# Batch 3's local q and k turned by DMA instead of the matrix engine, strided rows loaded in two pieces each, and a rearranged order of loads in a fused attention and MLP kernel

## The chip, the cores and the metric

The kernel runs on one core of a Trainium2 chip. The core has a matrix engine (PE, with its weight loads shown as PEld), two engines for elementwise work (DVE and ACT), a general engine that here mostly issues loads (POOL), an engine that here issues stores and DMA transposes (SP), and 16 DMA engines that move all of the data. The metric is the device time of one execution in microseconds (us); lower is better. Before the change it is 300.25 us, the median of three runs (299.5 to 300.93).

## The reference: strided sparse attention, then an MLP

The inputs q, k and v have the shape (8 batches, 8 heads, 576 positions, 64). Heads 0 to 3 are local: a position sees itself and the 31 before it. Heads 4 to 7 are strided: a position sees those at or before it that have the same remainder by 32, at most 18 of them. The attention's output is regrouped into 4608 tokens of 512 numbers, and goes through relu squared between two matrices.

```python
mask_local = (rel >= 0) & (rel < stride)
mask_strided = (rel >= 0) & (pos[None, :] % stride == pos[:, None] % stride)
...
attn = exp(where(mask, q @ k^T / 8, -1e9) - max);  out = (attn / sum) @ v
x = out.transpose(0, 2, 1, 3).reshape(4608, 512)
h = x @ w_in            # 512 x 2048
y = (relu(h) ** 2) @ w_out   # 2048 x 512
```

## The kernel before

**The MLP is the backbone.** The 4608 tokens are cut into 9 chunks of 512. For each chunk there are 16 groups of `mm1` (line 707: four matmuls of 128x128 on 512 columns, then relu on ACT and the square on DVE into `g_sb`) and 16 groups of `mm2` (line 729: four matmuls of 128x128 on 512 columns; every fourth ends an output tile that ACT copies to `y` and SP stores). That makes 288 groups, numbered through. The attention of a batch must be done, and its output stand in the `xt` tiles, before the `mm1` groups of the chunks that hold its tokens.

**The attention is woven in by hand.** The string `PLAN` says which attention steps are emitted ahead of which group, as `group: words`; a batch's two local head pairs are units 4b and 4b+1. The words that matter here:

- `l3k12+13`, `l3q12+13` (line 281): load the local k or q of batch 3, both units in one DMA, in rows of 1536 bytes, into room in `xt` that is not needed yet. `c12kv` and the like (line 294) copy one unit's rows into a `k_l` or `q_l` tile on DVE (`v`) or ACT (`a`). `T12ka` and the like (line 448) transpose them with six matmuls against an identity (line 453) and copy the result out of PSUM (line 460).
- `Q16k`, `Q16q` (line 273): load one unit's k or q straight into `k_l` or `q_l`, in two DMAs, in rows of 256 bytes. `Y16` (line 370) then transposes q and k with two DMA transposes that SP issues (line 378). Batches 4 to 7 go this way; batches 0 to 3 go the way of `l`, `c` and `T`.
- `C4q`, `C4k` (line 346): load the strided heads of a batch, 72 rows of 8 KB. `X4q`, `X4k` (line 352) transpose them by DMA from SP (line 354). `k40v`, `k41v` (line 361) copy the transposed k into the block-diagonal tile `kb` on DVE.
- `V4` (line 412) loads the local v of a batch into 128 partitions, 96 rows of each block and once more the 32 rows ahead of it, so that each block has its neighbours at hand. `U4` (line 388) loads the strided v in two DMAs: 54 rows of 8 KB for three heads (line 390), and 54 rows of 3 KB for the fourth (line 393), whose source is a three-level pattern. `B40v`, `B41v` (line 396) spread that into the tile `vb`.
- `S12!`, `D12.0`, `E12`: scores, the product with v, and the DMA transpose of the result into `xt` for a local unit. `G4` is the scores of both local units of a batch at once. `s3.0` and `x3.0` are scores and product with v for the strided heads.

**What sets the order.** Every engine runs its instructions in the order in which they are emitted, and waits where an operand isn't there. POOL issues all loads, in one line; SP issues all stores and DMA transposes, in one line. The tile framework gives the loads eight semaphores in turn, and the DMAs of SP eight others, so that a load isn't issued before the one eight places ahead of it has landed. Buffers: four `q_l`, four `k_l`, one `q_t` and one `k_t` for the strided rows (the next batch's `C` waits until the DMA transpose has read the last), one `v_st`, four `y`.

Of the kernel before, what the change touches and what calls it, by code (L numbers as in the profile page):

```python
# [82 lines left out]
77: s3.2  # L83
80: x3.0 B40v
81: B41v
82: x3.1
# [10 lines left out]
104: Y21 s4.1  # L97
105: D17.0
106: Q25k
107: B50v  # L100
# [6 lines left out]
116: x4.2  # L107
121: G5
124: V6
128: U6  # L110
133: D20.0
134: Y24 D20.1 X6k
# [8 lines left out]
144: x5.0  # L121
146: x5.1
149: x5.2
150: k60v
152: k61v
154: G6
156: V7
# [13 lines left out]
183: x6.2  # L141
188: G7 k70v
189: k71v
197: s7.0
198: D28.0 s7.1
199: D29.0
# [10 lines left out]
def kernel(  # L157
# [18 lines left out]
    NJ = 8  # L176
# [6 lines left out]
    NG = 5  # L183
# [116 lines left out]
    NP3 = 4 * SP_ // QL  # L300
    str_rows = {}

    def load_str_rows(b, name):
        src = q if name == "q" else k
        if b == 0:
            c = 4 if name == "q" else 8
            t = w_out_b[0:QL, c:c + NP3, :]
            nc.gpsimd.dma_start(out=t, in_=src[b, 4:8].rearrange("h (p j) d -> (h p) (j d)", j=NJ)
                                .rearrange("(s p) c -> p s c", p=QL))
        else:  # L310
            t = str_rows_t[name][0:SP_]
            nc.gpsimd.dma_start(out=t, in_=src[b, 4:8].rearrange("h (m r) d -> (h m) (r d)", r=STRIDE))
        str_rows[b, name] = t

    def step_TS(b, name, g, copy):
# [30 lines left out]
    def load_str_tall(b, name):  # L346
        src = q if name == "q" else k
        t = str_rows_t[name]
        nc.gpsimd.dma_start(out=t[0:SP_], in_=src[b, 4:8].rearrange("h (m r) d -> (h m) (r d)", r=STRIDE))  # L349
        big[b, name] = t  # L350

    def transpose_str(b, name):
# [252 lines left out]

    def load_v0():
        load_v_local_sw(0)
        nc.gpsimd.dma_start(
            out=vs0.rearrange("p u n d -> p (u n d)").rearrange("p (h c) -> p h c", h=4),
            in_=v[0, 4:8].rearrange("h (p j) d -> p h (j d)", j=NJ))  # L610

    def step_N(u):
        e, hw = st[u]["e"], S // 2
# [154 lines left out]
    def first_part(kks, ffs):  # L768
        for ff in ffs:
            mm1(0, ff, kks, FIRST, None if ff < 2 else "py")  # L770

    def run_step(word):
        word, _, at = word.partition("/")
        places[:] = [int(x) for x in at.split(",") if x]
        op, arg = word[0], word[1:]
# [206 lines left out]
```

## Time and profile before

| what | value |
|---|---|
| time, median of three runs (range) | 300.25 us (299.5 to 300.93) |
| time of the profiled execution | 298.88 us |
| its span, first to last instruction | 297.2 us |
| PE busy | 289.2 us, 97% |
| DVE, ACT, POOL busy | 177.9, 172.3, 72.4 us |
| granted PE clock | full over the span but for its last slices (0.96 from 290 us on) |
| DMA moved | 37.28 MB in 93131 packets |
| loads issued by POOL, DMAs issued by SP | 66 and 53 |

The profiled execution took 298.88 us, of which 297.2 us are its span and 1.7 us lie around it. A group of four matmuls takes about 0.865 us at full rate (216 ns from one start to the next). Group 16 starts at 33.3 us of the span, group 48 at 67.8, group 64 at 84.5, group 90 at 110.9.

### The profile page before, as it was taken

Reading aid. Unit: us, or ns where it says so; the run is one execution under the profiler, and the core shown is the slowest. Engines: PE = TensorE matmul, PEld = TensorE weight load, DVE = VectorE, ACT = ScalarE, POOL = GpSimd, SP = SyncE. Lnnn points to the kernel's source line nnn. Section 1 sums busy time; section 2 is a strip of 40 time slices with the busy share of each in tenths; the row PEclk is TensorE's granted clock in tenths of the full one; section 3 lists DMA queues with packets and bytes.
Section 4 is the critical chain, followed back from the end, with each engine's and each line's share of the span. In section 5 each row is a group of like instructions: output and inputs, shape, how many; then the busy total and the mean of one; then the engine's idle time right before and its main releaser. Section 6 shows DMA issues by size and latency. Waiting matters only on the chain.

```text
span 297.2 us, 5652 instructions
## 1 busy us (share of the span) xinstructions
PE 289.2 (97%) x2136; PEld 146.0 (49%) x2172; DVE 177.9 (60%) x460; ACT 172.3 (58%) x325; POOL 72.4 (24%) x105
## 2 busy tenths in 40 slices
PE   7999999999999999999999999999999999999996
PEld 2644555555544444544455445544554444444444
DVE  6866779677779694697267936785475534104400
ACT  3858846686667735783477447745665257217511
POOL 8846643006404027083303710000000000000000
PEclk9999999999999999999999999999999999999999
DMA  8999999999999999999999999521011100010012
GB/s 157 181 209 204 194 198 187 158 225 140 129 166 176 157 211 164 159 136 157 186 145 150 174 186 142 89 57 71 35 23 55 73 35 0 35 74 35 0 71 73
DMA packets 93131, 37.28 MB, mean 125 GB/s; under 512 B 78956, under 2 KB 87238, under 8 KB 93104
## 3 DMA queue, kind: packets, MB, share of 16 engines
q0 software_dynamic: 54448, 18.82, 58.1%
q1 hardware_dynamic: 38512, 18.03, 32.6%
q8 instruction: 17, 0.28, 0.4%
q14 instruction: 10, 0.08, 0.1%
q10 hardware_dynamic: 144, 0.07, 0.1%
HBM read 38.21 MB, written 9.44 MB: 160 GB/s over the span
## 4 chain that ended last, share of the span: by engine, by line
PE 92%; DVE 3%; ACT 2%; issue 2%; DVEq 0%; ACTq 0%
PE psb L729 39%; PE psb L707 39%; PE psb L667 2%; PE psb L453 1%; PE psb L764 1%; PE psb L588 1%; PE psb L505 1%; PE psb L754 1%; PE psb L585 1%; PE psb L574 1%; ACT r L713 1%; PE psb L550 1%; DVE g_sb L714 1%; PE psb L475 1%; PE psb L331 0%
## 5 line engine op out<-in xcount | busy, mean ns | idle before, releaser
L707 PE MATMUL psb<-xt,w_in_b 128*128 128x512 bf16 x558 | 132.1, 379 | 1.4 <-ACT xt L692 0.4
L729 PE MATMUL psb<-w_out_b,g_sb 128*128 128x512 bf16 x542 | 125.3, 379 | 1.3 <-issue 0.6
L713 ACT ACTIVATE r<-psb 128x512 bf16<-128x512 f32 x144 | 85.5, 600 | 37.5 <-PE psb L707 34.0
L714 DVE TENSOR_TENSOR g_sb<-r 128x512 bf16<-128x512 bf16 x144 | 60.7, 423 | 72.8 <-ACT r L713 71.7
L707 PEld LDWEIGHTS <-w_in_b 128*128 128x128 bf16 x576 | 53.4, 98 | 59.0 <-issue 1.6
L729 PEld LDWEIGHTS <-g_sb 128*128 128x128 bf16 x560 | 51.8, 98 | 57.2 <-DVE g_sb L714 0.3
L733 ACT COPY y<-psb 128x512 f32<-128x512 f32 x35 | 20.6, 589 | 53.2 <-PE psb L729 50.2
L598 DVE TENSOR_TENSOR xt<-psb,rv 64x144 bf16<-64x144 f32 x84 | 34.1, 406 | 8.0 <-ACT rv L591 6.8
L590 ACT ACTIVATE rv<-psb 128x432 f32<-128x432 f32 (+1 forms) x21 | 10.5, 501 | 9.8 <-PE psb L585 9.8
L673 DVE TENSOR_TENSOR x_l<-psb,rinv 96x384 bf16<-96x384 f32 x28 | 15.5, 554 | 1.0
L349 POOL DMA_DIRECT2D q_t<-in_q_dram x6 | 3.4, 567 | 43.4 <-DMA qT_s<-q_t 26.0
L604 DVE TENSOR_TENSOR xt<-psb,rv 64x270 bf16<-64x270 f32 (+1 forms) x28 | 10.9, 432 | 3.8 <-ACT rv L591 3.6
L575 ACT ACTIVATE e<-psb 128x432 bf16<-128x432 f32 (+1 forms) x21 | 10.4, 496 | 3.7 <-PE psb L574 3.7
L418 POOL DMA_DIRECT2D vl<-in_v_dram x7 | 10.3, 1475 | 8.6 <-DMA vl<-in_v_dram 6.2
L278 POOL DMA_DIRECT2D k_l<-in_k_dram x16 | 11.7, 736 | 2.8 <-PE psb L453 2.4
L278 POOL DMA_DIRECT2D q_l<-in_q_dram x16 | 11.6, 732 | 1.0 <-DMA k_l<-in_k_dram 1.0
L561 ACT ACTIVATE e<-psb 128x384 bf16<-128x384 f32 x24 | 9.6, 511 | 3.4 <-PE psb L550 3.4
L591 ACT ACTIVATE rv<-rv 128x432 f32<-128x432 f32 (+1 forms) x21 | 11.2, 533 | 0.7
L557 DVE TENSOR_TENSOR e<-e,mask_all 128x576 bf16<-128x576 bf16 x16 | 6.7, 459 | 7.2 <-ACT e L561 7.1
L667 PEld LDWEIGHTS <-e 128*128 128x128 bf16 x168 | 8.6, 101 | 4.6
L349 POOL DMA_DIRECT2D k_t<-in_k_dram x6 | 3.2, 535 | 28.0 <-DMA kT_s<-k_t 25.7
L667 PE MATMUL psb<-vl,e 128*128 128x65 bf16 x168 | 9.5, 195 | 0.1
(117 smaller groups left out, 215.9 us busy)
## 6 DMA issues: line engine op xcount, KB each, us to landing
out_dram<-y SPq DMA_DIRECT2D x35, 256.0 KB, 2.8
vl<-in_v_dram POOLq DMA_DIRECT2D x7, 384.0 KB, 12.4
w_out_b<-in_moe_w_out_dram POOLq DMA_DIRECT2D x4, 512.0 KB, 15.1
q_t<-in_q_dram POOLq DMA_DIRECT2D x7, 288.0 KB, 5.8
k_t<-in_k_dram POOLq DMA_DIRECT2D x7, 288.0 KB, 6.1
v_st<-in_v_dram POOLq DMA_DIRECT2D x7, 216.0 KB, 7.9
w_in_b<-in_moe_w_in_dram POOLq DMA_DIRECT2D x2, 704.0 KB, 13.1
k_l<-in_k_dram POOLq DMA_DIRECT2D x16, 72.0 KB, 8.1
```

What stands on the lines that cost most here:

```text
L278: nc.gpsimd.dma_start(out=t[:, :, hh, :], in_=src[b, 2 * p + hh].rearrange("(t p) d -> p t d", p=QL))
L590: nc.scalar.activation(rv, pn, AF.Ln)
L591: nc.scalar.activation(rv, rv, AF.Exp, scale=-1.0)
L598: nc.vector.tensor_tensor(to[:, :, NJ * part:NJ * (part + 1), par], of, by, op=ALU.mult)
L604: nc.vector.tensor_tensor(t, of[:, g:, :, lo:lo + k], by[:, g:, :, lo:lo + k], op=ALU.mult)
L667: nc.tensor.matmul(po[0:m, n, :], e[:, c:c + m], rhs[:, NL * part + n, 0:D + 1], start=True, stop=True)
L673: nc.vector.tensor_tensor(x, po[0:QL, :, 0:D], rinv[0:QL].to_broadcast([QL, NL, D]), op=ALU.mult)
L707: nc.tensor.matmul(ph, w_in_b[:, kk, 128 * ff:128 * (ff + 1)], xt[kk][:, 512 * c:512 * (c + 1)], start=(kk == order[0]), stop=(kk == order ...
L713: nc.scalar.activation(r, ph, AF.Relu)
L714: later(1, lambda: nc.vector.tensor_tensor(g[:, ff, :], r, r, op=ALU.mult))
L729: nc.tensor.matmul(py, g[:, ff, 128 * j:128 * (j + 1)], w_out_b[:, ff, :], start=(ff == 0), stop=(ff == 15))
L733: nc.scalar.copy(y, py)
```

## The change

Four things are done together.

1. Batch 3's local q and k are loaded with `Q` and transposed with `Y` on SP, as those of batches 4 to 7 are. The steps `l3k`, `l3q`, the four casts `c12*`, `c13*` and the four `T12*`, `T13*` go.
2. A load of 72 or 54 rows becomes two, one of the largest multiple of 16 rows and one of the rest (64 and 8, 48 and 6): `load_even`. The fourth head's v becomes three loads of 18 rows.
3. From batch 3 on the local v is loaded without the shared rows (96 partitions), and DVE copies the 32 rows across (`H3v` to `H7v`).
4. Loads of batch 4 are moved: `Q16*`, `Q17*` from groups 48 to 52 to group 56, behind `C4q`; `U4` from group 63 to 76, where it waits for the DMA transposes of `Y16` (`U4@Y16`); `Y17`, `Y16` from groups 66 and 67 to 76. `X2q` moves from group 31 to 26, ahead of `X2k`. Several steps of batches 3 and 4 shift by a few groups.

```diff
-22: B11v l3k12+13 s1.2 U2
+22: B11v Q12k Q13k s1.2 U2
-26: X2k l3q12+13 x1.1
+26: X2q X2k Q12q Q13q x1.1
-31: c8ka c9qv X2q
+31: c8ka c9qv
+40: Y12
-48: Q16k s2.0
+48: s2.0
-50: Q17q Q16q c12kv s2.1
-51: c12qa E9 s2.2
-52: Q17k c13kv c13qa
+50: s2.1
+51: E9 s2.2
+52: Y13
-56: x2.1 C4k C4q
-57: T12ka
-58: V4 T13qv T12qa
-59: T13ka
-60: x2.2 B30v
-61: B31v
-63: U4 S12!
+56: x2.1 C4q Q16k Q16q C4k Q17k Q17q
+57: H3v
+58: B30v V4
+59: B31v
+60: x2.2
+63: S12!
-66: Y17 k30v
-67: Y16 D12.1 S13! X4k C5q k31v
-68: C5k
-71: s3.0 E12 Q20k Q21q Q20q
-72: Q21k s3.1
-73: D13.0 D13.1
-75: E13
+67: D12.1 S13! C5q
+68: k30v
+69: k31v E12
+70: X4k
+73: D13.0 D13.1 s3.0
+75: s3.1 E13
+76: Y17 Y16 U4@Y16 C5k Q20k Q21q Q20q Q21k
...
+94: H4v
-97: Y20
+97: Y20 B40v Y21
...
+    def load_even(out, src):
+        n = out.shape[0] // 16 * 16
+        for r in (slice(0, n), slice(n, out.shape[0])):
+            nc.gpsimd.dma_start(out=out[r], in_=src[r])
...
-        nc.gpsimd.dma_start(out=t[0:SP_], in_=src[b, 4:8].rearrange("h (m r) d -> (h m) (r d)", r=STRIDE))
+        load_even(t[0:SP_], src[b, 4:8].rearrange("h (m r) d -> (h m) (r d)", r=STRIDE))
...
-        nc.gpsimd.dma_start(out=t[:, 0:RW], in_=v[b, 4:7].rearrange("h (m r) d -> (h m) (r d)", r=STRIDE))
-        src = v[b, 7]
-        src = bass.AP(src.tensor, src.offset, [[2 * NG * D, 3], [RW, NA], [1, 2 * (NG + 1) * D]])
-        nc.gpsimd.dma_start(out=t[:, RW:2 * NB * D], in_=src)
+        load_even(t[:, 0:RW], v[b, 4:7].rearrange("h (m r) d -> (h m) (r d)", r=STRIDE))
+        src = v[b, 7].rearrange("(m r) d -> m (r d)", r=STRIDE)
+        for g in range(3):
+            c = 2 * NG * D * g
+            nc.gpsimd.dma_start(out=t[NA * g:NA * (g + 1), RW:2 * NB * D], in_=src[:, c:c + 2 * (NG + 1) * D])
...
+        word, _, gate = word.partition("@")
...
+                if gate:
+                    tc.add_manual_dep(i, transfers[gate].name,
+                                      mybir.DependencyInfo(mybir.DependencyClass.Sync, mybir.DependencyReason.DATA),
+                                      reason="order of transfers")
...
-            load_v_local_all(int(arg))
+            (load_v_local_sw if int(arg) > 2 else load_v_local_all)(int(arg))
```

More of the change, by code (lines that the diff above doesn't have):

```diff
@@ L59 @@
 47: E8 D9.0 B21v U3
-48: Q16k s2.0
+48: s2.0
 49: D9.1
-50: Q17q Q16q c12kv s2.1
-51: c12qa E9 s2.2
-52: Q17k c13kv c13qa
+50: s2.1
+51: E9 s2.2
+52: Y13
 54: x2.0
 55: X3q X3k
-56: x2.1 C4k C4q
-57: T12ka
-58: V4 T13qv T12qa
-59: T13ka
-60: x2.2 B30v
-61: B31v
-63: U4 S12!
+56: x2.1 C4q Q16k Q16q C4k Q17k Q17q
[4 more added lines that the diff above has]
+63: S12!
 64: X4q
 65: D12.0
-66: Y17 k30v
-67: Y16 D12.1 S13! X4k C5q k31v
-68: C5k
-71: s3.0 E12 Q20k Q21q Q20q
-72: Q21k s3.1
-73: D13.0 D13.1
-75: E13
[L83 to L86, printed above, removed]
+67: D12.1 S13! C5q
[5 more added lines that the diff above has]
+76: Y17 Y16 U4@Y16 C5k Q20k Q21q Q20q Q21k
+78: s3.2
+81: x3.0
+83: x3.1
 85: x3.2
@@ L89 @@
 91: k41v
+94: H4v
 95: U5 D16.0 D16.1
-97: Y20
+97: Y20 B40v Y21
+98: B41v
 99: X5k
@@ L96 @@
 103: C6q s4.0
-104: Y21 s4.1
+104: s4.1
 105: D17.0
@@ L109 @@
 124: V6
+127: H5v
 128: U6
@@ L123 @@
 149: x5.2
-150: k60v
+150: k60v H6v
 152: k61v
@@ L143 @@
 189: k71v
+192: H7v
 197: s7.0
@@ L311, in load_str_rows @@
             t = str_rows_t[name][0:SP_]
-            nc.gpsimd.dma_start(out=t, in_=src[b, 4:8].rearrange("h (m r) d -> (h m) (r d)", r=STRIDE))
+            load_even(t, src[b, 4:8].rearrange("h (m r) d -> (h m) (r d)", r=STRIDE))
         str_rows[b, name] = t
@@ L607, in load_v0 @@
         load_v_local_sw(0)
-        nc.gpsimd.dma_start(
-            out=vs0.rearrange("p u n d -> p (u n d)").rearrange("p (h c) -> p h c", h=4),
-            in_=v[0, 4:8].rearrange("h (p j) d -> p h (j d)", j=NJ))
+        load_even(vs0.rearrange("p u n d -> p (u n d)").rearrange("p (h c) -> p h c", h=4),
+                  v[0, 4:8].rearrange("h (p j) d -> p h (j d)", j=NJ))
     def step_N(u):
@@ L770, in first_part, with run_word @@
             mm1(0, ff, kks, FIRST, None if ff < 2 else "py")
+    transfers = {}
     def run_step(word):
+        word, _, gate = word.partition("@")
+        traced = nc.cur_bb.bb.instructions
+        n = len(traced)
+        run_word(word)
+        for i in traced[n:]:
+            if "DMA" in type(i).__name__.upper() or "Dma" in str(getattr(i, "opcode", "")):
+                transfers[word] = i
+                if gate:
+                    tc.add_manual_dep(i, transfers[gate].name,
+                                      mybir.DependencyInfo(mybir.DependencyClass.Sync, mybir.DependencyReason.DATA),
+                                      reason="order of transfers")
+    def run_word(word):
         word, _, at = word.partition("/")
```

## The prediction

> **What bounds the kernel now.** I read the page's busy shares first, then its slices, then the chain of work that ended last, around the steps that the change removes.
>
> ```profile
> PE 289.2 (97%) x2136; PEld 146.0 (49%) x2172; DVE 177.9 (60%) x460; ACT 172.3 (58%) x325; POOL 72.4 (24%) x105
> PE   7999999999999999999999999999999999999996
> DMA  8999999999999999999999999521011100010012
> PE 92%; DVE 3%; ACT 2%; issue 2%; DVEq 0%; ACTq 0%
> ```
>
> PE is busy in every slice, and 92% of the chain is PE. Busy time alone proves little, so I went through PE's starts in order. A 512-column matmul starts 216 ns after the one before it. From 18 us to the end, nearly every longer step is one extra matmul of 216 ns, of which the trace lacks some records; what is left are some steps of 0.1 to 0.3 us behind score matmuls. So after the head PE waits for nothing, and the kernel gets shorter only by what PE no longer does. Against that, the DMA engines are full until about 190 us: a late load is what can make PE wait. The chain at the removed steps:
>
> ```profile
> 76.19 0.86 PE psb L729 x4
> 77.05 0.26 PE psb L453 x6
> 77.31 0.43 PE psb L729 x2
> ...
> 78.17 0.51 PE psb L453 x12
> 78.68 0.86 PE psb L729 x4
> 79.55 0.26 PE psb L453 x6
> ```
>
> Six transposes take 0.26 us of PE's own line, between matmuls that run back to back. Then the waits, the loads, and SP's line in the crowded stretch:
>
> ```profile
> POOL q_t L349 <- DMA qT_s<-q_t: 26.0, 2, 16.8
> SPq L354 <- DMA k_t<-in_k_dram: 49.9, 1, 49.9
> ...
> v_st<-in_v_dram POOLq DMA_DIRECT2D x7, 216.0 KB, 7.9
> v_st<-in_v_dram POOLq DMA_DIRECT2D x7, 81.0 KB, 8.2
> ...
> 51.73 2.75 SPq L354 DMA_TRANSPOSE kT_s<-k_t  x1
> 54.54 1.58 SPq L737 DMA_DIRECT2D out_dram<-y  x3
> 56.16 4.22 SPq L354 DMA_TRANSPOSE qT_s<-q_t  x1
> ...
> 64.94 0.37 DVE L365 COPY kb<-kT_s 64x864 bf16<-64x864 bf16 x1
> ```
>
> SP waits for batch 2's strided k until 51.7, issues its transpose, three stores, then q's transpose. They land 9.6 and 10.9 us after their starts, at 61.4 and 67.0. DVE wants k at 64.94, PE wants q at 67.6 (`s2.0`). These are the tightest places behind the head. POOL stands 16.8 us for the second transpose, which still reads `q_t`. The small v load takes as long as one 2.7 times its size: its 54 packets of 135 ns run, by their start times, as three rows of 18 one behind the other, so three DMA engines are held 2.4 us while the others are done.
>
> **The change, part by part.**
>
> *Transposes off PE.* `T12*`, `T13*`: 24 matmuls, 0.26 + 0.51 + 0.26 = 1.03 us of the chain. All of it is on the path. Nothing is added on PE. **-1.03 us.**
>
> *Casts and copies.* Four casts (DVE 0.35 each, ACT 0.83 each) and four copies out of PSUM (ACT 0.64 three times, DVE 0.76) go: 4.4 us off engines that are 60% and 58% busy. 0 on the path, since PE wasn't waiting for them.
>
> *Batch 3's loads.* Two of 288 KB become eight of 72 KB. POOL: 8 x 0.73 instead of 0.72 + 0.70, 4.4 us more on an engine 24% busy: 0. In the DMA queue, eight such loads landed between 115.7 and 119.8, 0.58 apart: 4.6 us of queue against about 3.5 for the two (1.7 and 1.8 behind the load before). About 1 us more, around 52 to 60. V3 behind them landed at 68.2 and is first wanted by `H3v` at group 57 (77.1): covered.
>
> *Four DMA transposes on SP.* Each takes 1.2 to 2.0 us to issue by line 378, so 5 to 8 us more in SP's line. `Y12` stands ahead of `E8` (66.9), whose wait for its operand lasts from 61 to 66.9 now: it fits in. `Y13` stands behind the store at 73.0 and ahead of `X3q`, `X3k`, which now start at 73.6 and 77.3 and take 3.6 and 4.6 us because eight `Q16`, `Q17` loads run beside them. Those loads come later in the new order, so I take 1.5 us an issue (lines 354 and 378 take 1.2 to 1.6 where no load runs): Y13, X3q, X3k from 73.5 to about 80, as now. Queued behind are stores; ACT has four `y` buffers and a `y` comes each 3.5 us. `S12!` (group 63, 83.8) and `S13!` (67, 88.1) have over 8 us of cover. 0.
>
> *Loads in pieces.* POOL issues 89 DMAs instead of 66. The nearest rows are 0.51 to 0.65 us an issue: 23 x 0.6 = 14 us, off the path. At the head one piece goes ahead of `w_in`: 0.5 us. The `w_in` loads land 7.9 to 14.7 us after their issue, behind a full queue, and the third lands at 20.6 for group 5 at 21.4: cover of 0.8, so 0. The gain: by the landing counts of each 72-row load one DMA engine is done up to 8 us before the rest and a second up to 4, the others hold five rows of 325 ns. With 64 + 8 that is four each and one more on eight. The 18-row pieces end the chains of 2.4 us. Around 50 us I expect landings 1 to 2 us earlier, bounds 0 and 2.5.
>
> *X2q ahead of X2k.* q landed at 50.0, k at 51.6. With q first the first transpose starts 1.6 us earlier and lands at about 59.8; k's follows without three stores between. Bounds for its landing: 61.4 (as now, when first) and 67.0 (as now, when second). The second one now needs 2.9 us beyond the store before it, so I take 59.8 + 3.5 = 63.3, nearest to the lower. DVE wants it at 64.94; behind that copy stands the mask that ends at 65.85 and that PE needs at 66.52, 0.67 us of cover more. So 0; at the upper end 67.0 - 64.94 - 0.67 = 1.4 us of stall. Below nothing is excluded: PE isn't waiting there now.
>
> *Local v without shared rows.* Five loads shrink by a quarter; each adds one DVE copy of 32x1280, 0.48 us by line 410: 2.4 us on DVE. The nearest deadline is `H3v`, between two long runs of line 598 and ahead of `x2.2`, where DVE has 1.32 us idle at 80.9 and has lost the 0.76 copy: 0.48 and the two `vb` copies moved up (1.04) fit. 0.
>
> *Held back rows.* `Q16`, `Q17` wait behind `C4q`, which waits for `X3q`, some 80 us; they land by about 91. `Y17`, `Y16` then stand behind `E13` (its operand is there at 96): four issues, landed by about 104, for `G4` at 110.9 (109.9 then). `U4` follows at about 104, wanted at group 97 (116.9). Now the last of these transposes lands at 108.2, so the cover grows. 0.
>
> Sum: 298.88 - 1.03 = 297.85 for an execution like the profiled one, span 296.2. The median stands 1.37 above the profiled time (300.25 - 298.88), so **299.2**.
>
> **The rivals.**
>
> *Loads evened out give more.* The median is 1.37 above the profiled execution, and the third and fourth quarter of `w_out` land at 42.9 and 47.0 for groups 24 and 28 at 43.2 and 47.6: an execution with slightly slower DMA would stall there, and the pieces make these landings earlier. If half to all of the 1.37 is such waiting, the time is 297.9 to 298.5; I say 298.2. Against: no trace of such an execution is here.
>
> *X2k late.* Up to 1.4 us of stall at `k20v`: 299.3 to 300.6, as bounded above.
>
> *The eight places run dry: slower.* A load waits for the landing of the one eight ahead, and pieces take places. The third and fourth `w_out` loads were issued at 28.7 and 31.7; now they wait for a piece of k (32.7) and for the second `w_out` load (37.7). If each still took its 14.2 and 15.3 us, the fourth would come at 53.0, 5.4 us after group 28 starts: 300.25 + 5.4 - 1.03 = 304.6. It decides from about 50 us on. Against: landings follow each other by size, not by issue (28.7, 29.5, 31.7 land at 42.9, 44.5, 47.0), and at 37.7 some 1.1 MB still stand in the queue, 6 us of work at 288 KB in 1.7 us.
>
> *Each piece costs a time of its own: slower.* Seven extra pieces stand ahead of or in batch 2's q. At 0.58 us each, as the 72 KB loads, q comes 4.1 us later, X2k at 67.4, and PE stalls 1.8: 301.0. If each held the queue for 3.9 us, the shortest time to landing of any 72 KB load, it is 27 us late and the time some 325. The Trainium skill, DMA: Bandwidth & Descriptors, Rules for kernel authors, speaks for this: small transfers should be merged, and under 64 KB one pays mostly overhead. By the 2.0 us of fixed cost that its section Anatomy of one DMA gives, the seven would be an estimated 14 us. The trace bears it out only where the queue is empty: full, landings come 0.58 us apart.
>
> **How the numbers follow.** Sum as worked out: 0.48 (299.2, and 298.7 to 299.9 by the scatter of the runs). Evened loads give more: 0.26. X2k late: 0.10. The eight places: 0.11. Pieces with a cost of their own: 0.05. A measurement of this kernel can tell about 0.5%, 1.5 us. Faster by over 0.5% is below 298.75: the second case and 0.06 of the first, 0.32. Slower is above 301.75: the eight places and 0.04 of the last, 0.15. Within: 0.53. The range leaves out the slower cases and the lowest edge of the second: 297.9 to 301.4, the upper end being 300.6 for X2k late with 0.7 for the scatter of the median (300.93 - 300.25).
>
> **What would show it.** Line 453's counterpart loses 24 of its 96 matmuls and PE's busy time falls by about 1 us (more by its own durations, which overlap); span near 296.2. Evened loads: strided rows and the fourth head's v land without stragglers, `w_out` no later than 42.9 and 47.0. X2k: k's transpose lands before 65, and DVE shows no wait there for `kT_s`. Wrong would be: a step over 0.3 us between PE's starts behind 18 us, ended by a load or transpose, above all at groups 24 to 28, 44 to 48, 63 and 90.

## The result and the profile after

The changed kernel takes 303.55 us, the median of six executions (301.39 to 305.9), against 299.93 for the kernel before (299.5 to 301.24). The ratio is 1.0116, with a 95% interval of 1.008 to 1.0151: it became slower by 1.2% where I had forecast no change that can be measured. Measured once more with ten executions on another chip it took 302.28 us (299.33 to 304.46) against 300.15. The change also made the time uneven: the executions of one set lie up to 5 us apart, those of the kernel before mostly within 2. The ratios given in this document leave out executions that lie more than 1.5% above the fastest of their kernel; since these late executions are what several of the edits cause, I give the median and the range over all executions, and read from those.

The lines of the page that answer to those shown of before (busy time; PE, granted clock and DMA in 40 slices of the span; shares of the chain that ended last):

```profile
PE 291.1 (97%) x2112; PEld 146.2 (49%) x2148; DVE 180.4 (60%) x462; ACT 169.7 (56%) x320; POOL 92.8 (31%) x147
PE   7799989999999999999999999999999999999995
PEclk9959999999999999999999999999999999999999
DMA  8999999999999999999998996711011110011011
PE 86%; DVE 5%; DMA 3%; ACT 2%; issue 2%; POOL 1%; DVEq 0%; ACTq 0%; POOLq 0%
```

POOL went from 105 instructions to 147: the traces hold 129 loads against 87, so the change adds 42, of which 36 are pieces (the 66 and 53 of the table ahead of the prediction are 87 and 79 in the trace). PE lost its 24 transposes (2136 instructions became 2112), and yet its busy time rose from 289.2 to 291.1: the clock row has a 5 in the third slice, where PE ran at half rate for 6.8 us. PE's share of the chain fell from 92% to 86%; DMA and DVE are on it now. By the starts of the groups, the profiled execution lost 3.5 us up to group 16 (33.35 became 36.87) and 1.0 at group 20, and won 1.0 between groups 56 and 60 (76.0 to 80.8 became 80.5 to 84.3), which are the removed transposes. The other 0.6 us of the span's 4.1 lie behind the landing of the last store.

The loss at the head, from the chain (start, us, what):

```profile
5.54 8.27 DMA vl<-in_v_dram
...
13.84 0.50 DVE vl L420
...
14.37 0.49 PE psb L657 x11
```

Batch 0's local v lands at 13.81 instead of 12.11. The products of line 657 need it: PE stands 0.66 us until it has landed and 0.31 us more for the DVE copy behind it (13.84); another 0.66 us it had stood before, at 8.6, for batch 0's strided k. By 14.7 us PE is 1.6 us behind the kernel before. From 14.8 us on the granted clock is 0.5 for 6.8 us, and at group 5 PE is 3.6 us behind: the halved clock cost 2 us, more than any of the waits.

The loss at group 20, on POOL and then on DVE (start, us, engine, line):

```profile
39.52 0.75 POOL L439 DMA_DIRECT2D w_out_b<-in_moe_w_out_dram  x1 [0.59 <-DMA w_out_b<-in_moe_w_out_dram]
40.26 1.29 POOL L887 MEMSET kb<- 128x1408 f32 x1
```

```profile
39.25 0.38 DVE L374 COPY kb<-kT_s 64x864 bf16<-64x864 bf16 x1
39.55 2.09 DVE L377 COPY kb<-kT_s 64x324 bf16<-64x324 bf16 x1
```

A copy that takes 0.24 us elsewhere takes 2.09 while POOL issues a load and clears `kb`; PE waits 0.83 us for what follows. Before, POOL issued the third and fourth quarter of `w_out` at 28.7 and 31.7 and cleared at 30.2 and 32.4, ahead of these copies; now it does so at 36.1, 39.5, 37.7 and 40.3.

SP's line in the crowded stretch, now with the four new transposes (`qT<-q_l` and `kTl<-k_l` at 67.7 to 79.5):

```profile
67.68 1.22 SPq L387 DMA_TRANSPOSE qT<-q_l  x1
69.01 1.90 SPq L387 DMA_TRANSPOSE kTl<-k_l  x1
71.40 6.00 SPq L691 DMA_TRANSPOSE xt<-x_l  x2
...
78.20 1.23 SPq L387 DMA_TRANSPOSE qT<-q_l  x1
79.47 1.32 SPq L387 DMA_TRANSPOSE kTl<-k_l  x1
80.96 1.32 SPq L363 DMA_TRANSPOSE qT_s<-q_t  x1
82.40 2.09 SPq L363 DMA_TRANSPOSE kT_s<-k_t  x1
...
101.28 3.51 SPq L387 DMA_TRANSPOSE qT<-q_l  x1
104.90 1.22 SPq L387 DMA_TRANSPOSE kTl<-k_l  x1
106.22 1.21 SPq L387 DMA_TRANSPOSE qT<-q_l  x1
107.48 1.27 SPq L387 DMA_TRANSPOSE kTl<-k_l  x1
```

In this execution nothing behind 43 us makes PE wait over 0.35 us. But the last four (batch 4's local rows) land at 109.4 to 110.9, where I had said about 104, and the scores that need them don't wait, starting at 113.8, because PE is 3.5 us late by then. The other executions show what that means.

### The profile page after: what moved, and what is told of

Same layout as the page of the kernel before. It is cut to its first block, busy times and chain, and to the rows that moved or that the text cites. A ratio compares the mean times of both kernels' runs of the same rounds, so it can differ in the third digit from the quotient of the medians.

```text
span 301.3 us, 5671 instructions
## 1 busy us (share of the span) xinstructions
PE 291.1 (97%) x2112; PEld 146.2 (49%) x2148; DVE 180.4 (60%) x462; ACT 169.7 (56%) x320; POOL 92.8 (31%) x147
## 3 DMA queue, kind: packets, MB, share of 16 engines
q1 hardware_dynamic: 40944, 18.62, 32.1%
## 4 chain that ended last, share of the span: by engine, by line
PE 86%; DVE 5%; DMA 3%; ACT 2%; issue 2%; POOL 1%; DVEq 0%; ACTq 0%; POOLq 0%
PE psb L716 38%; PE psb L738 38%; DMA vl<-in_v_dram 3%; PE psb L676 1%; PE psb L598 1%; ACT r L722 1%; PE psb L584 1%; PE psb L763 1%; DVE g_sb L723 1%; PE psb L595 1%; PE psb L560 1%; DVE kb L377 1%; PE psb L698 1%; DVE e L537 1%; DVE kb L374 1%
## 5 line engine op out<-in xcount | busy, mean ns | idle before, releaser
L281 POOL DMA_DIRECT2D k_l<-in_k_dram x20 | 14.8, 746 | 8.1 <-DMA k_t<-in_k_dram 2.2
L281 POOL DMA_DIRECT2D q_l<-in_q_dram x20 | 14.8, 750 | 4.2 <-DMA v_st<-in_v_dram 2.1
L310 POOL DMA_DIRECT2D q_t<-in_q_dram x14 | 7.7, 558 | 26.0 <-DMA qT_s<-q_t 25.5
L310 POOL DMA_DIRECT2D v_st<-in_v_dram x14 | 7.4, 534 | 21.3 <-DVE vb L407 10.7
L614 DVE TENSOR_TENSOR xt<-psb,rv 64x270 bf16<-64x270 f32 (+1 forms) x28 | 10.9, 430 | 2.5 <-ACT rv L601 2.2
L403 POOL DMA_DIRECT2D v_st<-in_v_dram x21 | 10.7, 517 | 4.2 <-DMA w_out_b<-in_moe_w_out_dram 2.3
L310 POOL DMA_DIRECT2D k_t<-in_k_dram x14 | 7.5, 549 | 12.0 <-DMA kT_s<-k_t 7.5
## 6 DMA issues: line engine op xcount, KB each, us to landing
w_in_b<-in_moe_w_in_dram POOLq DMA_DIRECT2D x2, 704.0 KB, 13.3
```

What stands on the lines that cost most here:

```text
L281: nc.gpsimd.dma_start(out=t[:, :, hh, :], in_=src[b, 2 * p + hh].rearrange("(t p) d -> p t d", p=QL))
L310: nc.gpsimd.dma_start(out=out[r], in_=src[r])
L614: nc.vector.tensor_tensor(t, of[:, g:, :, lo:lo + k], by[:, g:, :, lo:lo + k], op=ALU.mult)
```

## The experiments

The times over the kernel before are differences of medians over all executions of the same chip; the last column has the ratio, with its 95% interval, by the rule given above. "Whole" or "pieces" is how the strided rows are loaded; "PE" or "DMA" is how batch 3's local q and k are transposed.

| run | loads | batch 3 | median (range), us | over before, us | ratio (95% interval) |
|---|---|---|---|---|---|
| after_again | pieces | DMA | 302.28 (299.33 to 304.46) | +2.1 | 1.0053 (1.0018 to 1.0088) |
| v0_whole | pieces but for batch 0 | DMA | 303.99 (302.31 to 304.47) | +3.8 | 1.0124 (1.0088 to 1.0159) |
| whole_to_batch1 | pieces from batch 2 | DMA | 302.07 (299.58 to 308.02) | +2.0 | 1.0012 (0.9967 to 1.0056) |
| plan_only | whole | DMA | 304.90 (299.27 to 308.57) | +4.8 | 1.0024 (0.9985 to 1.0063) |
| y_as_before | whole | DMA | 306.85 (300.56 to 313.55) | +6.7 | 1.0070 (1.0020 to 1.0119) |
| y13_behind | whole | DMA | 308.75 (304.14 to 311.63) | +9.1 | 1.0206 (1.0141 to 1.0271) |
| dma_transposes_alone | whole | DMA, old plan | 305.56 (302.56 to 309.62) | +5.4 | 1.0134 (1.0085 to 1.0182) |
| pieces_only | pieces | PE, old plan | 303.58 (301.62 to 304.88) | +3.4 | 1.0115 (1.0061 to 1.0168) |
| pieces_pe | pieces | PE | 301.88 (300.66 to 304.12) | +1.9 | 1.0064 (1.0038 to 1.0091) |
| memsets_first | pieces | PE | 303.42 (302.47 to 303.61) | +3.8 | 1.0110 (1.0087 to 1.0133) |
| tiny_pieces | whole, and tiny extra loads | PE | 301.84 (301.74 to 303.02) | +2.2 | 1.0075 (1.0052 to 1.0098) |
| pe_transposes | whole | PE | 299.48 (299.20 to 300.46) | -0.6 | 0.9987 (0.9971 to 1.0003) |
| rows_only | whole | PE, rows as for DMA | 300.75 (299.31 to 301.30) | +0.8 | 1.0013 (0.9993 to 1.0033) |
| idle_transposes | whole | PE, and four idle DMA | 300.32 (299.43 to 303.81) | +0.4 | 1.0028 (0.9995 to 1.0062) |
| rows_and_idle | whole | PE, both of these | 302.73 (300.52 to 309.63) | +3.1 | 1.0086 (1.0055 to 1.0117) |

**The changed kernel once more.**

> The changed kernel once more, unaltered, for a second profile of it. Theory H (the loss lies in the loads in pieces, in the first 45 us): 302 to 305 us; batch 0's local V lands after 13 us again, PE stops for about 1 us there, and the groups of batch 0 start 3 to 4 us later than in the kernel before; the copy of batch 1's k at line 377 takes about 2 us again beside POOL's memsets. Rival S (scatter of one execution's DMA engines): the time is near 302 but the profile has no stop at 13 us, and the loss sits elsewhere. Rival P (the plan of 50 to 110 us): a step of PE's starts behind 50 us.

The time is as expected by H, the place only in part. The head lost 1.0 us (the local v landed at 13.2; the clock stayed at 1.0). The copy of line 377 was slow once more, 1.39 us beside the clear of `vb`, but this time PE did not have to wait for it. Instead PE stood 1.4 us at 111.9, ahead of group 90, a step behind 50 us as rival P had it. The chain there (start, us, what):

```profile
97.84 6.62 DMA q_l<-in_q_dram
...
104.52 2.38 SPq L387
...
107.00 1.21 SPq L387
...
108.31 1.21 SPq L387
...
109.58 3.66 DMA kTl<-k_l
...
113.28 0.68 PE psb L560 x24
```

Batch 4's rows come late, SP issues their four transposes one after another, the last lands at 113.2, and the scores of line 560 wait for it. So different executions of one kernel lose in different places.

**Batch 0's strided v in one load again**, and **whole loads up to batch 1**:

```diff
-        load_even(vs0 ..., v[0, 4:8] ...)
+        nc.gpsimd.dma_start(out=vs0 ..., in_=v[0, 4:8] ...)
```

> The changed kernel with batch 0's strided V in one transfer, as in the kernel before; all other loads stay in pieces. Theory H, head part: if this piece is what makes the local V late, batch 0's groups start as in the kernel before (group 16 at about 33.5 instead of 36.9 us) and the time falls to 299.5 to 300.5 us, the rest of the loss (0.9 us at group 20) staying. If the late V is not this piece's doing: 302 to 304 us, unchanged.

> The changed kernel with whole loads for batches 0 and 1 (strided V of batch 0, strided q, k and V of batch 1) and pieces from batch 2 on. If the loss of the head (1.0 us at group 0 in the second profile of the changed kernel, 3.6 in the first) is made by the pieces there: groups 0 to 20 start as in the kernel before (within 0.3 us), and the time is that of the changed kernel less 1 us or more, 300 to 303 us, the stop at group 110 staying. If the head's loss comes from scatter: 302 to 304 us.

In both the head is near its old place (group 0 at 16.4 us in both; 15.8 before, 18.7 and 16.8 in the changed kernel, group 5 at 21.6 and 22.0). In neither did the time fall: PE waits at 110 us for batch 4's `kTl`, 1.1 and 2.1 us. Over five profiles with batch 0's v in pieces its local v lands at 12.5 to 13.8 us, mean 13.3; over fifteen with it whole at 12.1 to 13.3, mostly 12.3 to 12.8. The head's share of the loss is thus likely the piece's doing, but with this overlap it is not shown, and it isn't what decides the median.

**The pieces alone, and the plan alone.** The first puts `load_even` and the 18-row loads into the kernel before; the second takes them out of the changed kernel:

```diff
-        for r in (slice(0, n), slice(n, out.shape[0])):
-            nc.gpsimd.dma_start(out=out[r], in_=src[r])
+        nc.gpsimd.dma_start(out=out, in_=src)
```

> The kernel before, with the strided loads in even pieces and the shared part of strided V in three pieces of 18 rows; its plan, its PE transposes of batch 3 and its local V stay. Theory H: slower than before by 3 to 4.5 us, 303 to 305 us, with the same stop at 13 us and the same 0.9 us at group 20. Rival P (the plan is to blame): 299.5 to 300.5 us, as before.

> The changed kernel with every strided load in one transfer, as in the kernel before: batch 3's DMA transposes, the local V without shared rows and the later order of loads stay. Theory H: the step of 1.03 us that 24 PE transposes cost is all that is left, 298.6 to 299.4 us. Rival P: 302 to 304 us, slower than before.

Each alone is slower than the kernel before: the pieces by 1.15% (ratio 1.0115, 1.0061 to 1.0168), the plan by 4.8 us in the median, with executions from 299.27 to 308.57. The ratio of the plan alone is not clear of 1; what shows its loss is how often it is late: 7 of its 10 executions lie above 303 us, and 2 of 94 of the kernel before. H is right on the time of the first and wrong on the second, which it had at 299. It is wrong on the place, too: in the profile of `pieces_only` PE loses no time at the copy into `kb`, but stands 2.0 us at 68.6 for batch 2's strided q, whose transpose is late. The profiled execution of the plan alone is one of the two best: groups 56 to 60 take 3.8 us, and its last copy out of PSUM ends 0.3 us before that of the kernel before (its time is 0.7 longer all the same, since the last stores land later). So the step of 1.03 us exists, and in most executions something larger eats it.

**Which part of the plan.** Three edits: batch 4's local rows back where they were; batch 3's transposes back on PE; and only batch 3's DMA transposes, in the kernel before.

```diff
 y_as_before
-56: x2.1 C4q Q16k Q16q C4k Q17k Q17q     +48: Q16k ...  50: Q17q Q16q ...  52: ... Q17k
-76: Y17 Y16 U4@Y16 ...                   +66: Y17   67: Y16 ...
 pe_transposes
-22: ... Q12k Q13k   26: ... Q12q Q13q   40: Y12   52: Y13
+22: ... l3k12+13    26: ... l3q12+13    50 to 52: c12*, c13*   57 to 59: T12*, T13*
 dma_transposes_alone
 the reverse of pe_transposes, on the kernel before
```

> The changed kernel with whole loads (as the run with the plan alone), and batch 4's local rows loaded and transposed at the groups of the kernel before (loads 48 to 52, transposes 66 and 67, ahead of batch 4's strided k on SP). Theory Q (what stretches the plan alone is SP's queue: batch 4's local k stands behind X4q, the two stores of batch 3's outputs and X4k, lands at 108.4 us in the best case where group 110's scores need it at about 110, and is late in most executions): the spread of 299.3 to 308.6 us closes to within 1.5 us of the kernel before, median 298.6 to 300 us. Rival T (the four DMA transposes of batch 3 delay the queue by themselves): still 302 to 306 us with the wide spread.

> The changed kernel with whole loads, and batch 3's local q and k on TensorE again (cast loads and 24 transposes as in the kernel before); local V without shared rows and the held-back rows of batch 4 stay. Theory Q: SP loses four transfers ahead of batch 3's strided transposes, but batch 4's transposes stay behind X4k: stalls at group 110 in some executions, 300 to 303 us. Rival T: the spread closes, and the time is the kernel before's plus 0 to 0.5 us, 300 to 300.7 us.

> The kernel before with only batch 3's local q and k by four DMA transposes (their rows loaded in bf16 a head at a time, transposes issued at groups 40 and 52), nothing else. Theory Q: minus the 1.03 us of 24 transposes on PE: 298.8 to 299.6 us, narrow. Rival T: wide, median 301 to 305 us, with a stop of PE at group 110 for batch 4's k or at group 64 to 73 for batch 3's.

Theory Q falls, rival T stands, though each of the three times lies 0.5 to 0.9 us outside its range. With PE transposes and everything else of the plan, the kernel takes 299.48 us in a narrow range, ratio 0.9987 (0.9971 to 1.0003), and none of its 11 executions is above 303: the local v without shared rows, the held-back rows and the order of X2 together cost nothing. With the four DMA transposes and their rows as the only edit it takes 305.56. `y_as_before` says less than its time: its one profile (304.05) lost 5.0 us before group 20, of which 0.85 us are a wait for batch 0's k at 8.7 and most of the rest is the halved clock behind it, all ahead of the four transposes, and PE never waited for a DMA transpose. Where its later executions lose is not seen. The waits of PE in the profile of `dma_transposes_alone` (309.62):

```profile
PE psb L573 <- DVE kb L364: 4.6, 1, 4.6
PE psb L706 <- DMA xt<-x_l: 1.9, 1, 1.9
...
PE psb L504 <- DMA kTl<-k_l: 1.2, 1, 1.2
```

All three are DMA transposes that land late: unit 8's output 17.1 us after SP began to issue it (68.1 to 85.2), batch 3's strided k at 98.2, unit 13's k at 91.6. What the DMA engines did from 70 to 90 us, first there, then with PE transposes:

```profile
DMA  9719998999981499595899985999999999959999
GB/s 132 8 9 144 218 235 155 179 201 60 26 26 17 11 95 86 59 135 73 117 131 139 123 88 71 77 75 94 67 52 110 274 212 128 77 51 150 150 147 125
DMA packets 6382, 2.16 MB, mean 108 GB/s; under 512 B 6001, under 2 KB 6055, under 8 KB 6381
```

```profile
DMA  9220946999921228999990099992697999999999
GB/s 145 25 31 0 115 74 115 166 145 72 38 25 28 37 39 228 359 291 291 301 52 5 10 280 380 397 381 25 78 180 123 160 128 131 151 217 297 192 176 174
DMA packets 7094, 3.03 MB, mean 151 GB/s; under 512 B 6371, under 2 KB 6425, under 8 KB 7092
```

With PE transposes the queue runs empty now and then in this stretch. With the DMA transposes it hardly does, and moves 2.16 MB instead of 3.03 in the same time.

**Rows, transposes, or waiting.** The rows of the change loaded but transposed on PE; PE transposes and cast loads, plus four DMA transposes that nobody reads; both additions; and unit 13's transposes behind batch 3's strided ones on SP.

```diff
 rows_only            Q12*, Q13* kept; T12*, T13* read those tiles; no Y12, Y13
 idle_transposes      pe_transposes, and at groups 40 and 52 two DMA transposes each into a spare tile
 rows_and_idle        rows_only, and the same idle transposes
 y13_behind           -52: Y13   -55: X3q X3k   +55: X3q X3k Y13
```

> The changed kernel with whole loads; batch 3's rows are loaded as in the change, in eight loads of 72 KB in 128-byte packets, but transposed on TensorE (24 transposes), not by DMA. Theory R (the eight loads in small packets, 3936 packets more in the queue of the loads, are what makes the rest late): 301 to 305 us and a wide spread. Theory T2 (the transposes themselves, on SP and on the DMA engines): 299.3 to 300.5 us, narrow.

> The kernel with batch 3's transposes on TensorE and whole loads (299.5 us), plus four DMA transposes of the same size whose result nobody reads, issued by SP at groups 40 and 52 from rows that are there. Theory T2 (the transposes take DMA engines and SP's line, whoever needs them): 301 to 305 us and wide. Theory W (what costs is waiting for their data: SP stands before them for their rows, with the rest queued behind): 299.3 to 300.5 us, narrow, as without them. Theory R: the same as W.

> Batch 3's rows in eight loads of 128-byte packets and PE transposes (300.75 us), plus the four DMA transposes that nobody reads, from rows that are there. All DMA work of the change's batch 3 is done, but nothing waits for the transposes, and SP stands before none of them for its rows. Theory M (the DMA engines are full until 190 us, so the added engine time of 8 + 5 us delays every later load): 303 to 306 us and wide, like the plan alone. Theory W (SP's waiting order): 300.5 to 301.5 us, about the sum of the two single additions.

> The changed kernel with whole loads (304.9 us over all executions, 299.3 to 308.6), with unit 13's two DMA transposes moved behind batch 3's strided q and k on SP's line. Theory W (SP's order: unit 13's transposes stand ahead of X3q and X3k, whose reading of q_t and k_t holds batch 4's loads): the spread closes, median 299 to 300.5 us. Theory M: the spread stays, median 302 to 306 us.

By the medians the rows cost 0.8 us against the kernel before, or 1.3 against `pe_transposes` (299.48, on another chip), and the idle transposes 0.4 or 0.8; neither ratio is clear of 1, and R and T2, which had 301 to 305 us for one of the two alone, are both wrong. Both together, with nothing waiting for what the transposes write, give +3.1 and executions up to 309.63. That is clear of noise, nearer to M (303 to 306) than to W (300.5 to 301.5), and more than the sum, though the excess over the sum is hardly clear of the scatter. In the late execution that was profiled (309.07) PE stands 4.1 us at 87.0 at the end of this chain:

```profile
74.55 15.45 DMA v_st<-in_v_dram
...
90.57 0.47 DVE qT L475
...
91.08 0.63 PE psb L522 x11
```

Batch 3's strided v, a plain load, lands 15.4 us after its issue; in `pe_transposes` the same load takes 6.4. DVE stands for it, with the copy that PE wants queued behind, and none of the four added transposes is in the chain: the added work makes other transfers late. Putting unit 13's transposes behind does not help: `y13_behind` is the slowest of all, and in its profile PE stands 6.2 us for the moved transpose itself. What the order does is to choose who is late. Against `pe_transposes` the rows put 3936 more packets into the loads' queue (50608 became 54544) in exchange for nothing, since the bytes are the same; the transposes put 2432 more into SP's (38512 became 40944). The kernel before had 54448 in the loads' queue: over the whole kernel the smaller local v gives back nearly what the rows add (3840), though four of its five loads come behind 90 us. By 60 us the loads had moved 9.71 MB with the small rows and 10.09 without: at some 180 GB/s, 2 us behind.

**Apart and together, in the quiet end of the kernel.** To the kernel with PE transposes I added transfers that nobody reads, behind 240 us: the change's four transposes (T) alone, loads alone, then all together.

```diff
+230: T alone, loads alone     (three_kinds: loads alone)
+262: T and loads together
 apart_together: two local v loads   apart_strided: two strided loads   three_kinds: two of each
```

> The kernel with TensorE transposes and whole loads, with extra transfers that nobody reads in its last stretch, where the DMA engines are nearly idle: at about 243 us four DMA transposes of one unit pair (the size of the change's four) alone, behind them two local V loads of 288 KB in 128-byte packets alone, and at about 271 us the same four transposes and the same two loads together. Theory M2 (transposes and loads in small packets slow each other far beyond sharing): together they take over 1.3 times the sum of the two times alone, and their packets last over 1.5 times as long as alone. Theory M1 (they only share the engines): together no longer than the sum, packets under 1.3 times. The time itself should stay at 299 to 300.5 us.

> As the run before it, with two strided loads of 288 KB (72 rows, 4096-byte packets, the form of batch 4's strided q and k) in place of the local V loads: four DMA transposes alone at 241 us (6.5 us), the two loads alone behind them, and all six together at 271 us. The loads alone should take 5 to 6 us from the first issue to the last landing. Theory M4 (it is transposes beside 4096-byte packets that make the rate collapse to 50 to 110 GB/s in the slow executions): together over 14 us, the loads' packets over 600 ns against about 325 alone. Theory M1 (the kinds only share the engines): together 7 to 11 us, packets under 450 ns.

> The same quiet stretch, with two local V loads and two strided loads, alternating, alone at about 243 us, and at about 271 us once more together with the four transposes. Theory M1: alone about 10 us, together no more than the sum with the transposes' 6.5, so up to 16.5 us. Theory M4 or M5 (three kinds at once collapse): together over 18 us, at 60 to 110 GB/s.

Times from the first issue to the last landing, in one execution each: T alone 6.5 us, one transpose each 1.3 us. Local v loads alone 7.2, together with T 11.6. Strided loads alone 6.5, together 9.4. So two kinds share the engines, and less than the sum is needed, as M1 said. Their packets grew more than M1 had it: the transposes' from 20 to 35 ns beside local v loads, those of 4096 bytes from 377 to 465 beside T. All three kinds: loads alone 10.9 us, with T 17.2 (M1 had 16.5 at most); the sum is 17.4. In that full queue four transposes cost 6.3 us, nearly the 6.5 that they take alone, one after the other. Alone their packets are an estimated 2.9 us of the 16 engines' time (2304 packets of 20.4 ns), in the full queue 6.0 (of 41 ns), so the price can't be read from the quiet case. The landings of the loads in `three_kinds`, alone and then with the transposes (KB each, median us from issue to landing):

```profile
vl<-in_v_dram POOLq DMA_DIRECT2D x2, 288.0 KB, 6.7
...
k_t<-in_k_dram POOLq DMA_DIRECT2D x1, 288.0 KB, 8.0
```

```profile
vl<-in_v_dram POOLq DMA_DIRECT2D x2, 288.0 KB, 12.1
...
k_t<-in_k_dram POOLq DMA_DIRECT2D x1, 288.0 KB, 13.8
```

By their packets in the trace, those of 128 bytes last 32 ns alone and 60 on the average with all kinds at once, those of 4096 bytes 331 and 449; the transposes' of 256 bytes 20 and 41. M4 and M5 had over 18 us, which isn't reached. Single microseconds fall to 47 GB/s. In the late executions the rate stays low for longer: from 75 to 85 us it averages 78 GB/s in `dma_transposes_alone` and 87 in `rows_and_idle` (118 in the kernel before, 171 in `pe_transposes`), from 70 to 80 us 95 in `y13_behind` (133 and 126). Why it does is left open.

**What the pieces cost.** The changed kernel with only batch 3's transposes back on PE; that, with POOL's two clears moved ahead of `w_out`'s third quarter; and whole loads with PE transposes, but behind each load that the change cuts as many loads of 8 x 2 elements as the cut would add.

```diff
 memsets_first
-6: o2 l2k8+9 mv0g o3 mk0g
+6: mv0g mk0g o2 l2k8+9 o3
 tiny_pieces (36 such loads into a spare tile)
+            nc.gpsimd.dma_start(out=spare[:, c:c + 2], in_=q[0, 0, 0:8, 0:2])
```

> The changed kernel with only its DMA transposes of batch 3 undone (cast loads and PE transposes as in the kernel before); the loads in pieces stay. With whole loads the same undoing gave 299.5 us and a narrow spread. Theory U (two independent causes: the four DMA transposes with their rows, and the pieces): 301.5 to 304 us, with 0.5 to 1 us lost at the head and a stop near group 48 for batch 2's q, or at group 20 for DVE's copy. Rival V (pieces hurt only beside the DMA transposes): 299.2 to 300.2 us.

> The changed kernel with PE transposes for batch 3 and the loads in pieces (301.9 us), with POOL's two memsets of the second pair of blocks (vb, kb) moved ahead of the third quarter of w_out in its line, so that they end before DVE copies batch 1's strided k. Theory D (in this kernel the pieces cost by the collision of POOL's memsets with DVE at 37 to 41 us, seen as 1.4 us of stops at groups 16 to 20): 300.0 to 301 us, and no stop at 38 to 41 us. Theory L (the pieces cost by the loads coming later): 301.5 to 302.5 us.

> The kernel with PE transposes and whole loads (299.5 us), plus, behind every load that the change cuts, as many loads of 8 x 2 elements as the cut would add (into a spare tile). Same number of DMAs on POOL and same use of the eight places in flight as with pieces, but each large load stays whole. Theory N (the count costs: places, POOL's time): 301 to 302.5 us, with the third and fourth w_out loads issued at 35 us or later instead of 31.7. Theory E (the cut itself costs, the way the rows lie over the engines): 299.3 to 300.3 us.

Pieces cost 2.4 us against `pe_transposes` without any DMA transposes of batch 3, so U is right and V wrong. Tiny loads that move next to nothing cost about the same, so the number of loads is enough, however the rows lie over the engines. Their profile shows where: POOL issues the third and fourth quarter of `w_out` 7 us later than with whole loads (29.3 and 32.6 there). Of the 7.4 us that the third quarter loses, 5.4 are more waiting for landings, since each load needs one of the eight places, and 2.1 the issue of four tiny loads.

```profile
29.18 0.55 POOL L406 DMA_DIRECT2D v_st<-in_v_dram  x1 [1.46 <-DMA xt<-in_k_dram]
...
33.29 0.50 POOL L312 DMA_DIRECT2D spare<-in_q_dram  x1 [1.70 <-DMA w_out_b<-in_moe_w_out_dram]
...
36.68 0.80 POOL L447 DMA_DIRECT2D w_out_b<-in_moe_w_out_dram  x1 [0.27 <-PE psb L523]
...
38.20 1.39 POOL L895 MEMSET vb<- 128x1408 f32 x1
39.53 0.75 POOL L447 DMA_DIRECT2D w_out_b<-in_moe_w_out_dram  x1
40.28 1.29 POOL L895 MEMSET kb<- 128x1408 f32 x1
```

All that stands behind is late too. Batch 2's strided k lands at 67.7 instead of 65.1; DVE stands for it, and PE for DVE:

```profile
DVE kb L381 <- DMA kT_s<-k_t: 1.7, 1, 1.7
```

```profile
PE psb L684 <- DVE e L545: 1.2, 1, 1.2
```

Theory D, that the clears beside DVE's copies are the loss, is not enough. With the clears ahead, the stop at 40 us is gone from the profile (0.9 us in `pieces_pe` and 0.3 in `tiny_pieces`), but `w_out`'s third quarter goes out at 38.0, batch 2's strided k lands at 69.3, and the kernel takes 303.42, more than either theory had. In the profile the late k costs 0.8 us; the other 3.4 us of the groups' delay are there at group 5, ahead of the moved clears, made by a late local v (13.7) and the clock at half rate for 6.8 us from 14.75 on, as in the changed kernel. The other four executions have a clock of 0.999 or 1.0 and take 302.47 to 303.61; where they lose is not seen.

## Why the prediction was wrong

The forecast was 299.2 us, with a range of 297.9 to 301.4 (its upper end adds up to 301.3) and no change over 0.5%; it is 303.55. Two steps that the sum had at 0 failed, the four DMA transposes on SP and the loads in pieces. Each makes the kernel slower when it is added alone (`dma_transposes_alone` +5.4, `pieces_only` +3.4), and the time of before comes back when both are out (`pe_transposes`, -0.6). The two don't add up, and how much of the changed kernel's loss belongs to which is open: with the pieces in, taking the transposes out gives nothing back that can be measured (`pieces_pe` +1.9, the changed kernel +2.1 when measured once more); with whole loads it gives back 5.4.

- *Transposes off PE, -1.03.* Right. Groups 56 to 60 take 3.7 to 3.8 us instead of 4.8 in the changed kernel (both profiles), `v0_whole`, `plan_only` and `whole_to_batch1`.
- *Casts and copies, 0.* Nothing speaks against it; the waits that I found have other causes. (The eight sum to 5.0 us by the figures given, not 4.4.)
- *Batch 3's loads, "about 1 us more, around 52 to 60", covered.* Mis-sized. The loads fall 2 us behind by 60 us. Alone they cost 0.8 to 1.3 us by the medians, which is not clear of noise; in the profile of `rows_only` batch 2's k lands at 67.2 and PE stands 1.2 us, the stop for which I had 1.4 us as an upper bound. I worked the price out from the spacing of landings in the tail of a burst, and not from packets.
- *Four DMA transposes on SP, 0.* The first step that failed. I counted what they take of SP's line, 5 to 8 us, and found room for it. I did not count what they take of the 16 DMA engines, which I had called full until 190 us a few lines above. In a full queue they took 6.3 us, and in the late executions what stands behind them and their rows in the DMA engines comes later still: in `dma_transposes_alone` batch 3's strided k lands at 98.2 and unit 8's output at 85.2, in `pe_transposes` at 82.7 and 71.8. With their rows, as the only edit, they give 305.56. The four transposes without the rows cost nothing clear of noise (`idle_transposes`), so it is the two together that fill the engines.
- *Loads in pieces, 0.* The second step that failed. I had 23 more loads (89 instead of 66) and 14 us of POOL; the traces have 42 more (129 instead of 87, 6 of them batch 3's rows), and POOL was busy 20.4 us longer. The time of POOL was put down as off the path, but POOL's line with eight places in flight decides when the loads go out. Number alone costs 2.2 us. The gain from evened loads was not seen: with PE transposes the pieces cost 2.4 us. With the DMA transposes the kernel with pieces came out lower than without (+2.1 against +4.8), but these ranges overlap over 5 us, and I leave it open.
- *X2q ahead of X2k, 0; local v, 0; held-back rows, 0.* Right in the sum: `pe_transposes` holds all three and loses nothing. The landings were forecast too early all the same. X2k landed at 65.1 there (63.3 forecast), batch 4's rows at 98.0 (91), and its transposes at 107.9 (104), no earlier than in the kernel before (108.2), so the cover did not grow. With batch 3's DMA transposes they landed at 108.4 in one of the two best executions of `plan_only`, at 110.9 and 113.2 in the two profiles of the changed kernel, at 111.5 in `v0_whole` and 112.8 in `whole_to_batch1`; in the last three PE stood 1.1 to 2.1 us for them. Holding the rows back left no room for that.
- *The rivals.* Eight places run dry: its first half came true (loads at 36.1 and 39.5 us), its second not, for they landed 1.2 and 1.1 us later only, with no stop at groups 24 to 28; the price was paid by POOL's other work and batch 2's k. Each piece costs a time of its own: 301.0 was near what pieces alone with PE transposes give (301.88), though I had it at 0.05. That is partly luck, since it had the pieces take time of the DMA queue, and `tiny_pieces` loses as much with next to nothing in the queue. The rule that I set aside there, in the Trainium skill, DMA: Bandwidth & Descriptors, section Rules for kernel authors, to merge small transfers, had the sign right; the runs show 0.06 us a load (2.2 us for 36), mostly through the places in flight, and no 2 us each.
- *The sum against one execution.* I took cover of 0.7 to 8 us from one execution of a kernel whose loads vary by a microsecond from one execution to the next, and in a full queue each lateness is handed on.

The version with PE transposes and whole loads, 299.48 us, is the only one with a median below that of the kernel before; that it is faster is not shown (its interval reaches 1.0003).

## What to carry to other kernels

Where the DMA row reads 9 for a long stretch, the DMA engines are an engine with its own line: a transfer added there can make everything behind it late, however free the queue that issues it is. Take the price from a full queue, and in packets rather than bytes. Count loads as well as bytes where a fixed number may be in flight: 36 loads of almost nothing cost as much as cutting the real ones into 36 more. Before trusting cover of a few microseconds, look at how far the landings move between executions.

## What was not expected of the hardware

**Transposes beside loads.** Alone, a DMA transpose of 147 KB lands every 1.3 us and its packets of 256 bytes last 20 ns. In the queue of three kinds they last 41 ns, and the others' packets 1.4 to 1.9 times as long as alone. The Trainium skill, DMA: Bandwidth & Descriptors, section Issuing engines are not separate DMA queues, says that DMAs of all issuers run on the same 16 engines and interleave; 17.2 us together against 17.4 one after the other agrees with it. No run here gives the reason for the 78 to 95 GB/s over 10 us in the late executions.

**The clock.** In the changed kernel PE stood 0.66 and 0.31 us around 13.5 us, and the clock was halved for 6.8 us from 14.8 on (in `memsets_first` 0.72 and 0.31, and the same 6.8 us); in `y_as_before` a single idle of 0.85 us at 8.7 was followed by 10.2 us at half rate from 11.9. In `after_again` 0.22, 0.31 and 0.38 us of idle in the same place left it at 1.0, and so did the 1.9 us wait at 85 us in `dma_transposes_alone`; a wait of 4.6 us at 95.7 there was followed by 3.4 us at half rate. In `rows_and_idle` the clock was halved 2.2 us into a wait of 4.1 us (87.0 and 89.2). The Trainium skill, TensorE: Matmul & The Clock Gate, Part 1, has the clock drop after an idle window of about 3.4 us. The wait of 4.6 us agrees, the others don't: 2.2 us of idle among long matmuls came before a drop, and at the head, where PE runs many short matmuls, under 1 us did. Which measure of activity decides was not tried.

**DVE beside POOL.** A copy of 0.24 us took 2.09 while POOL issued a load and cleared a tile. In `after_again`, `v0_whole`, `pieces_pe` and `tiny_pieces` the same copy took 1.38 to 1.39 us beside the clear of `vb`, and ended 0.1 us behind it. The Trainium skill, SBUF — State Buffer, section SBUF: two separate sides, calls the port pair that both use an exclusive lock: a DVE operation in a mode that takes two ports and a POOL operation block each other, and the later one waits for the whole of the other. Whether this copy runs in such a mode, no row here shows. The ends just behind the clears fit it, and so do the 2.09 us, being about as long as POOL's two instructions (0.75 and 1.29). That every load issued by POOL holds up a copy is not seen: at 42.0 to 42.6 in the changed kernel the two copies took their 0.38 and 0.24 us beside one.
